# Attention with sinks and a gated network on one core: the sinks' product in 64 weight columns, late value products reordered, a new step order

## The chip, the cores and the metric

One core of one Trainium2 chip runs the whole program. The metric is the device time of one execution in microseconds (us). The kernel before took 727.1 us, the median of 3 runs (726.25 to 728.53).

## The reference

```python
scores = scale * np.matmul(q, k.transpose(0, 1, 3, 2))      # 4 batches, 8 heads, 768 x 64
keep = is_sink | in_window                                  # first 4 keys, or the last 128
a = np.exp(np.where(keep, scores, -1e9) - max); a = a / (sum + 1e-9)
attn_out = np.matmul(a, v)
x = attn_out.transpose(0, 2, 1, 3).reshape(3072, 512)
h = x @ w_in                                                # 512 x 2048
out = (h * np.cos(h)) @ w_out                               # 2048 x 512
```

All of it is fp32; the weights arrive as 64-bit floats.

## The kernel before, in words

Every fp32 product that needs accuracy is made of three fast products: an operand is split into a rounded high part and a rest (fp32r), and high x high, high x low and low x high are summed in PSUM.

The 768 query rows of a batch are worked in chunks of 256 rows (`CB` = 2 blocks of 128). `chunks` lists first the four chunks at row 0 (the early heads, 32 of them: chunk and head), then the other two chunks of each batch (the late heads, 64 of them, 16 for each batch). Two chunks make a pair, and each of the 6 pairs then goes through the dense network in 16 slots (`dense_pair`): 12 matmuls of 512 columns into `h` (L476), sine and gate on ACT and DVE, 12 matmuls into `acc` (L521).

A late head takes scores against its window blocks and 8 sink keys (L1024), a mask with the row minimum (L1046), an exponential (L1055), a normalisation (L1075), a transpose of the probabilities (L1136), a split into high and low (L1162, L1167) with two triangular selections on POOL (L1174), and the value product `values` (L1215). That one is 7 matmuls into one PSUM tile `av` of 128 x 256. The stationary operand (the weights, loaded by LDWEIGHTS, on rows PEld) is the value block: 128 columns (`v` high and `v` low side by side) against the high probabilities, or its 64 high columns against the low ones. The moving operand has 256 columns for the key block that both query blocks see (wide) and 128 for the two others (narrow). In the order of before: wide high, the sinks, narrow high, narrow low, wide low, narrow high, narrow low.

The sinks' matmul serves 4 heads from one moving tile `gt`: `sink_cols` (L1105, L1107) gathers the sinks' probabilities of 4 heads into 16 rows each, high and low; `sink_turn` transposes (L1120) and `sink_out` copies to `gt`. Its weights `sink_values()` lie in the tile `x1r`. Each batch makes them once: `load_batch_v` (L852 to L861) issues 8 DMAs from SP into `xb`, and `vs_part` (L1091, four times) splits them with two DVE (or POOL) instructions each. `xb` is one buffer: the low half of each late head's value product also goes through it (`x_low` L1222, `x_sum` L1234), so a batch's load starts after the `x_sum` of the head before, and the first head's `x_low` comes after the four `vs_part`.

The order is not written by hand. Each step is added with engines and guessed durations, dependencies, buffers and a priority worked out from constants in `C`; `Plan.order` plays a list schedule and emits the instructions in its order of starts. Each engine then runs its own list in order. A load of 4 planner units (`dma(4)`) counts 1.8 us of SP there, and a `vs_part` 0.55 us of DVE. In gaps of the plan PE gets filler matmuls (`fill`, L1532, up to 60).

Of the kernel before, what the change touches and what calls it, by code (L numbers as in the profile page):

```python
# [9 lines left out]
F32 = mybir.dt.float32  # L10
# [8 lines left out]
SW = P + NSINK  # L19
GR = 96 + 2 * NSINK  # L20
BW = 2 * P + NSINK
# [5 lines left out]
C = {  # L27
# [4 lines left out]
    "POOLF": 0.999, "POOLPEN": 2.492, "R": 2, "RAW": 2, "SAME": 0.056, "SEM": 0.352, "SPE": -0.019, "STEP": 7.601,  # L32
# [3 lines left out]
}  # L36
# [136 lines left out]
def attn_moe_kernel(ctx, tc, q, k, v, n_sink, window, w_in, w_out, out):  # L173
# [50 lines left out]
    neg3 = cp.tile([P, 4], F32, name="neg")  # L224
    neg, quarter = neg3[:, 0:2], neg3[:, 2:3]
    lims = cp.tile([1, 2, 2, 2], F32, name="lims")
# [6 lines left out]
    def setup():  # L233
# [8 lines left out]
        nc.gpsimd.iota(rc_i[:, 0], pattern=[[-1, P]], base=0, channel_multiplier=1)  # L242
        nc.gpsimd.iota(rc_i[:, 1], pattern=[[1, P]], base=0, channel_multiplier=0)
        nc.vector.memset(ones, 1.0)
        nc.vector.memset(quarter, HALF_PI_DOWN)
# [9 lines left out]
        nc.vector.tensor_single_scalar(out=minus, in_=ident, scalar=-1.0, op=ALU.mult)  # L255
        nc.vector.tensor_copy(out=rc, in_=rc_i)
        nc.vector.tensor_single_scalar(out=env.below, in_=rel, scalar=0.0, op=ALU.is_lt)

# [537 lines left out]
    def banded_path(ctx2):  # L796
# [33 lines left out]
        def x1r():  # L830

            if env.x1r is None:
                env.x1r = ap.tile([P, NP * NT], F32R, name="x1r", tag="x1")
                env.vs = env.x1r.rearrange("p (a b c d) -> p a b c d", a=NP, b=2, c=2)
            return env.x1r
# [16 lines left out]
        def load_batch_v(o):  # L852
            def fn(e):
                o.vs32 = xb[:, : 2 * D].rearrange("p (n d) -> p n d", d=D)
                for h in range(4):
                    for dup in range(2):
                        r0 = h * 32 + dup * 8
                        nc.sync.dma_start(
                            out=o.vs32[r0 : r0 + 8], in_=v[o.b, h::4, 0:NSINK, :].rearrange("p s d -> s p d")
                        )  # L860
            return fn  # L861
# [229 lines left out]
        def vs_part(o, h):  # L1091
            def fn(e):
                w = sink_values().rearrange("p (g a) b c d -> p g (a b) c d", g=2)
                r = slice(h * 32, h * 32 + 2 * NSINK)
                e.tensor_copy(out=w[r, :, h, 0, :], in_=o.vs32[r])
                e.tensor_tensor(
                    out=w[r, :, h, 1, :], in0=o.vs32[r], in1=f32(w)[r, :, h, 0, :], op=ALU.subtract
                )
            return fn

        def sink_cols(o, four):
            def fn(e):
                j0 = o.sj[0]
                for h, oo in enumerate(four):
                    nc.vector.tensor_copy(out=gc.bitcast(F32R)[:, j0:, h * 32 : h * 32 + NSINK], in_=oo.p[:, j0:, P:SW])  # L1105
                for h, oo in enumerate(four):
                    nc.vector.tensor_tensor(  # L1107
                        out=gc[:, j0:, h * 32 + NSINK : h * 32 + 2 * NSINK], in0=oo.p[:, j0:, P:SW],
                        in1=gc[:, j0:, h * 32 : h * 32 + NSINK], op=ALU.subtract,
                    )  # L1110
            return fn
# [4 lines left out]
        def sink_turn(o):  # L1116
            def fn(e):
                o.gp = late_bank(o, 2)[:GR]
                for n, j in enumerate(o.sj):
                    nc.tensor.transpose(  # L1120
                        out=o.gp[:, n * P : (n + 1) * P], in_=gc[:, j], identity=ident,
                    )
            return fn

        def sink_out(o):
            def fn(e):
                w = len(o.sj) * P
                copy(e, gt[:GR, :w], o.gp[:, :w])
            return fn
# [66 lines left out]
        def values(o):  # L1196


            def fn(e):
                o.av = late_bank(o, 1)  # L1200
                mms = {}
                for t, w in ((o.phi, 2 * D), (o.plo, D)):
                    for n, (kb, qs) in enumerate(o.cols):
                        dst = o.av[:w, (qs[0] - o.i0) * P : (qs[-1] + 1 - o.i0) * P]
                        lhs = o.vr[:, kb - o.kb0].rearrange("p a d -> p (a d)")[:, :w]
                        mms.setdefault((w, len(qs)), []).append((dst, lhs, t[:, o.offs[n] * P : o.offs[n + 1] * P]))
                (wide_hi,), (wide_lo,) = mms[2 * D, CB], mms[D, CB]
                narrow = [m for pair in zip(mms[2 * D, 1], mms[D, 1]) for m in pair]
                seq = [wide_hi]
                if o.sj:  # L1210
                    lhs = sink_values()[:, o.pair, o.odd].rearrange("p a d -> p (a d)")
                    seq.append((o.av[:, o.sj[0] * P :], lhs, gt[:, : len(o.sj) * P]))
                seq += [*narrow[:2], wide_lo, *narrow[2:]]
                for n, (dst, lhs, rhs) in enumerate(seq):
                    nc.tensor.matmul(  # L1215
                        out=dst, lhsT=lhs, rhs=rhs, start=(n == 0), stop=(n == len(seq) - 1), skip_group_check=True
                    )
# [64 lines left out]
        def before_softmax(g, o):  # L1282
# [35 lines left out]
            if o.early:  # L1318
                if o.odd == 0:
# [3 lines left out]
                    i = add(dma(2), load_natural(xq_t, src, CB), [bx], pq, lat=2.3 if g else 1.9)  # L1323
                    i = qt = add([("PE", 0.23)], pe_turn(o, 0, xq_t, CB), [i, bb], t - 6 * T + C["DQ"] + 0.3)
                    bx.users.append(i)
# [105 lines left out]
        def after_softmax(g, o):  # L1431
            x, t = xs[o.a], head_time(g)
            if o.first is o:
                o.bv, o.bvs = buf("xb", 1), buf("vs", 1)
                i = add(dma(4), load_batch_v(o), [o.bv], t - 3 * T, lat=2.3)
                d = [i, o.bvs]
# [256 lines left out]
        ps = env.ps = ctx2.enter_context(tc.tile_pool(name="ps", bufs=1, space=PSUM))  # L1693
        gc = ap.tile([P, CB, GR], F32, name="gc")
        env.x1f = ap.tile([P, NP, PT], F32, name="x1f", tag="x1")
# [157 lines left out]
```

## Time and profile before

| what | before |
|---|---|
| median of 3 runs | 727.1 us |
| span of the profiled execution, first to last instruction | 725.6 us |
| PE (matmul) busy | 708.8 us, 98% |
| DVE, ACT, POOL busy | 599.3, 527.7, 127.5 us |
| granted clock of PE | 0.999 |

The trace counts from the first instruction. The profiled execution's own time is not given apart from its span; the span is 1.5 us below the median of the runs. A matmul's end in the trace is modelled, and matmuls overlap, so a matmul's cost is read from the distance between its start and the next one's start.

### The profile page before, as it was taken

The page shows a single profiled execution, that of the slowest core. Times are in us where ns is not written, and L with a number is a line of the kernel's source. Part 1 is how long each engine was busy: PE and PEld are TensorE (multiplying, and loading weights), DVE is VectorE, ACT ScalarE, POOL GpSimd, SP SyncE. Part 2 cuts the span into 40 slices and gives each one's busy share as a digit, 9 for nine tenths or more (in the row PEclk, how much of TensorE's full clock was granted, in tenths as well). Part 3 has the DMA queues.
Part 4 walks back from the last instruction along what each step waited for, and adds up shares of the span by engine and source line. Part 5 has one row for each costly group of instructions (what it writes and reads, how often), then busy time and mean ns, then how long its engine had stood idle before and what let it go on. Part 6 is the DMA issues. An engine that isn't in the chain of part 4 may idle for free.

```text
span 725.6 us, 12986 instructions
## 1 busy us (share of the span) xinstructions
PE 708.8 (98%) x3674; PEld 584.1 (81%) x3674; DVE 599.3 (83%) x1849; ACT 527.7 (73%) x1344; POOL 127.5 (18%) x213
## 2 busy tenths in 40 slices
PE   7998999999999999999999999999999999999996
PEld 7766787888888888888888888888888888888884
DVE  6889998988988978988978988878989865667762
ACT  3896976788697697796686886776887766566642
POOL 1010000001223222232231222232123222100000
PEclk9999999999999999999999999999999999999999
DMA  5665555533256333355433254433254500375551
GB/s 144 182 186 153 158 162 162 141 65 68 68 118 146 73 62 57 72 119 124 93 60 59 56 131 103 118 61 64 43 139 99 119 18 12 97 210 148 164 137 64
DMA packets 236501, 77.13 MB, mean 106 GB/s; under 512 B 221060, under 2 KB 221060, under 8 KB 236420
## 3 DMA queue, kind: packets, MB, share of 16 engines
q1 hardware_dynamic: 236128, 75.15, 43.4%
q10 hardware_dynamic: 292, 1.05, 0.5%
q8 instruction: 32, 0.52, 0.3%
q14 instruction: 49, 0.40, 0.2%
HBM read 69.86 MB, written 6.29 MB: 105 GB/s over the span
## 4 chain that ended last, share of the span: by engine, by line
PE 81%; ACT 11%; DVE 4%; issue 2%; DMA 1%; SPq 0%; ACTq 0%; DVEq 0%
PE acc L521 32%; PE h L476 32%; PE av L1215 5%; PE s L1024 4%; ACT p L1055 3%; PE s L968 2%; PE av L1191 2%; PE tp L1136 2%; ACT p L1073 1%; PE tp L1146 1%; PE qk L931 1%; ACT L485 1%; PE idle L1532 1%; ACT L1055 1%; ACT early L390 1%
## 5 line engine op out<-in xcount | busy, mean ns | idle before, releaser
L521 PE MATMUL acc<-whi_out,ghi 128*128 128x512 f32 x384 | 161.8, 421 | 0.0
L476 PE MATMUL h<-xhi,whi_in 128*128 128x512 f32 x384 | 155.2, 404 | 0.0
L476 PE MATMUL h<-xlo,whi_in 128*128 128x512 f32 x384 | 150.9, 393 | 0.0
L521 PE MATMUL acc<-whi_out,glo 128*128 128x512 f32 x384 | 150.8, 393 | 0.0
L521 PE MATMUL acc<-wlo_out,ghi 128*128 128x512 f32 x384 | 150.1, 391 | 0.0
L476 PE MATMUL h<-xhi,wlo_in 128*128 128x512 f32 x384 | 150.0, 391 | 0.0
L1174 POOL TENSOR_SCALAR_AFFINE_SELECT ph<-ph 128x512 fp32r<-128x512 f32 x128 | 87.4, 683 | 230.3 <-DVE ph L1167 226.4
L485 ACT ACTIVATE r<-h 128x512 f32<-128x512 f32 x96 | 57.1, 598 | 48.6 <-PE h L476 46.0
L476 PEld LDWEIGHTS h<-xlo,whi_in 128*128 128x128 f32 x384 | 72.1, 188 | 16.3
L521 PEld LDWEIGHTS acc<-whi_out,glo 128*128 128x128 f32 x384 | 72.1, 188 | 16.2
L476 PEld LDWEIGHTS h<-xhi,whi_in 128*128 128x128 f32 x384 | 72.2, 188 | 12.0 <-DVE r L498 0.3
L476 PEld LDWEIGHTS h<-xhi,wlo_in 128*128 128x128 f32 x384 | 72.4, 189 | 11.2
L521 PEld LDWEIGHTS acc<-whi_out,ghi 128*128 128x128 f32 x384 | 72.8, 190 | 10.7
L521 PEld LDWEIGHTS acc<-wlo_out,ghi 128*128 128x128 f32 x384 | 72.7, 189 | 9.4
L1055 ACT ACTIVATE p<-p,st 128x136 f32<-128x136 f32 (+1 forms) x192 | 79.2, 416 | 0.3
L498 DVE SCALAR_TENSOR_TENSOR r<-r,h 128x512 f32<-128x512 f32 x96 | 64.6, 674 | 16.9 <-ACT r L491 16.1
L506 ACT CAST ghi<-r 128x512 fp32r<-128x512 f32 x96 | 59.5, 619 | 22.8 <-PE acc L521 15.7
L512 DVE TENSOR_TENSOR glo<-r,ghi 128x512 fp32r<-128x512 f32 x96 | 66.3, 691 | 7.1 <-ACT ghi L506 6.3
L1046 DVE CUSTOM_DVE_ANT_0 p<-s,mk 128x136 f32<-128x136 f32 (+1 forms) x192 | 59.8, 313 | 6.5 <-PE s L968 3.1
L984 ACT CAST l<-tq 64x256 fp32r<-64x256 f32 x64 | 25.8, 403 | 46.7 <-PE s L1024 46.4
L1032 DVE COPY_PREDICATED s<-mk,s 128x128 f32<-128x128 int32 x128 | 37.3, 291 | 24.6 <-PE s L1024 22.5
L1024 PEld LDWEIGHTS s<-r,l 128*128 128x128 f32 x256 | 46.5, 188 | 12.3 <-DVE ph L1167 1.5
(153 smaller groups left out, 1302.3 us busy)
## 6 DMA issues: line engine op xcount, KB each, us to landing
xk<-in_k_dram SPq DMA_DIRECT2D x256, 48.0 KB
raw<-in_moe_w_out_dram SPq DMA_DIRECT2D x16, 512.0 KB
wt<-in_moe_w_in_dram SPq DMA_DIRECT2D x32, 256.0 KB
raw<-in_moe_w_in_dram SPq DMA_DIRECT2D x14, 512.0 KB
v<-in_v_dram SPq DMA_DIRECT2D x64, 96.0 KB
raw<-in_v_dram SPq DMA_DIRECT2D x32, 192.0 KB
out_dram<-wt SPq DMA_DIRECT2D x22, 256.0 KB
wt<-in_moe_w_out_dram SPq DMA_DIRECT2D x20, 256.0 KB
```

The costliest lines, as they stand in the source:

```text
L476: nc.tensor.matmul(out=o.h, lhsT=w[:, c, fs], rhs=xx[:, c, :], start=(c == 0 and n == 0), stop=(c == NC - 1 and n == 2),)
L485: nc.scalar.activation(out=o.r, in_=o.h, func=AF.Sin, scale=0.5)
L498: nc.vector.scalar_tensor_tensor(out=o.r, in0=o.r, scalar=0.5, in1=o.h, op0=ALU.subtract, op1=ALU.mult)
L506: nc.scalar.copy(out=o.ghi, in_=o.r)
L512: e.tensor_tensor(out=o.glo, in0=o.r, in1=f32(o.ghi), op=ALU.subtract)
L521: nc.tensor.matmul(out=y.acc[j], lhsT=gg[:, j * P : (j + 1) * P], rhs=w[:, f, :], start=(f == 0 and n == 0), stop=(f == NFT - 1 and n == 2),)
L1024: nc.tensor.matmul(out=o.s_ps[j][:, :w], lhsT=o.l[:, j * P : (j + 1) * P], rhs=r.rearrange("p n s -> p (n s)")[:, c0 : c0 + w], start=(n = ...
L1032: nc.vector.copy_predicated(out=o.s_ps[j][:, :P], mask=below.bitcast(I32), data=o.s_ps[j][:, SW : SW + P])
L1046: nc.vector.tensor_tensor_reduce(out=o.pj[j][:, :w], in0=o.s_ps[j][:, :w], in1=masks[min(o.i0 + j, 2)][:, :w], op0=ALU.add, op1=ALU.min, s ...
L1055: nc.scalar.activation(out=o.pj[j][:, :w], in_=o.pj[j][:, :w], func=AF.Exp, bias=o.lead.st[:, 0, o.nth, j : j + 1], scale=-1.0, accum_out= ...
L1174: nc.gpsimd.affine_select(out=ph[:, :, b, :], in_=f32(ph)[:, :, 1, :], pattern=[[0, 2 * CB], [(-1, 1)[b], P]], compare_op=(ALU.is_gt, ALU. ...
L1215: nc.tensor.matmul(out=dst, lhsT=lhs, rhs=rhs, start=(n == 0), stop=(n == len(seq) - 1), skip_group_check=True)
```

## The change

1. `vs_part` and `load_batch_v`: the values of the sinks stand in 4 copies instead of 2 (16 DMAs of 8 rows for a batch, before 8). Of each head's 32 rows, 16 hold the high part and 16 the rest; both lie in the same 64 columns. `vs_part` takes 3 instructions on 32 rows instead of 2 on 16. Setup makes the sign that it needs (`odd16`).
2. `sink_cols` writes each probability part twice (32 rows for each head); `gc` has 128 columns instead of 112, and the transposes and copies cover 128 rows.
3. `values`: the sinks' weights have 64 columns instead of 128, and the order is narrow high, narrow low, sinks, narrow high, narrow low, wide low, wide high.
4. The load of the first batch's sink values depends on the last early pair's q transposes on PE.
5. Most of the planner's constants in `C` have new values.

```diff
             def fn(e):
                 o.vs32 = xb[:, : 2 * D].rearrange("p (n d) -> p n d", d=D)
                 for h in range(4):
-                    for dup in range(2):
+                    for dup in range(4):
...
         def vs_part(o, h):
             def fn(e):
-                w = sink_values().rearrange("p (g a) b c d -> p g (a b) c d", g=2)
-                r = slice(h * 32, h * 32 + 2 * NSINK)
-                e.tensor_copy(out=w[r, :, h, 0, :], in_=o.vs32[r])
-                e.tensor_tensor(
-                    out=w[r, :, h, 1, :], in0=o.vs32[r], in1=f32(w)[r, :, h, 0, :], op=ALU.subtract
-                )
+                r = slice(h * 32, h * 32 + 32)
+                w = sink_values()[r, :, h // 2, h % 2, :]
+                e.tensor_copy(out=w, in_=o.vs32[r])
+                e.tensor_scalar(out=w, in0=f32(w), scalar1=odd16[r], scalar2=1.0, op0=ALU.mult, op1=ALU.mult)
+                e.tensor_tensor(out=w, in0=f32(w), in1=o.vs32[r], op=ALU.add)
...
-                (wide_hi,), (wide_lo,) = mms[2 * D, CB], mms[D, CB]
-                narrow = [m for pair in zip(mms[2 * D, 1], mms[D, 1]) for m in pair]
-                seq = [wide_hi]
-                if o.sj:
-                    lhs = sink_values()[:, o.pair, o.odd].rearrange("p a d -> p (a d)")
-                    seq.append((o.av[:, o.sj[0] * P :], lhs, gt[:, : len(o.sj) * P]))
-                seq += [*narrow[:2], wide_lo, *narrow[2:]]
+                sinks = o.av[:D], sink_values()[:, o.h // 4, o.pair % 2, o.odd], gt
+                seq = [
+                    block(0, o.phi, 2 * D), block(0, o.plo, D), sinks, block(2, o.phi, 2 * D),
+                    block(2, o.plo, D), block(1, o.plo, D), block(1, o.phi, 2 * D),
+                ]
...
-                    i = qt = add([("PE", 0.23)], pe_turn(o, 0, xq_t, CB), [i, bb], t - 6 * T + C["DQ"] + 0.3)
+                    i = qt = env.turned = add([("PE", 0.23)], pe_turn(o, 0, xq_t, CB), [i, bb], t - 6 * T + C["DQ"] + 0.3)
...
-                i = add(dma(4), load_batch_v(o), [o.bv], t - 3 * T, lat=2.3)
+                i = add(dma(4), load_batch_v(o), [o.bv] + ([env.turned] if o.b == 0 else []), t - 3 * T, lat=2.3)
...
-    "DV": 0.57, "DX": 4.638, "FILL": 60, "CV": 1.947, "CL": 15.777, "HO": -18.522, "SX": -5.15, "CR": 9.813,
+    "DV": 0.435, "DX": 5.298, "FILL": 60, "CV": 9.941, "CL": 26.879, "HO": -25.153, "SX": -5.111, "CR": 8.062,
...
-    "T": 6.724, "TH": 7.177, "WARM": 5, "WARM2": 0, "P0": 12.442, "A0": -3.102, "D0": 9.766, "G0": 3.059,
+    "T": 6.674, "TH": 7.389, "WARM": 5, "WARM2": 0, "P0": 13.606, "A0": -4.046, "D0": 12.406, "G0": -0.285,
...
-    "WO": 8.749, "WS": 1.523, "WS2": 1.141, "WT": 2, "XV": 2, "VP": 3.149,
+    "WO": 9.561, "WS": 0.201, "WS2": 1.447, "WT": 2, "XV": 2, "VP": -8.681,
```

`VP` shifts the priority of `vs_part`, `HO` that of all late heads; no guessed duration of a changed step has a new value.

## Rows read from the trace of the kernel before

**Rows 1.** The page: busy us, share of the span and instructions of each engine.
```profile
PE 708.8 (98%) x3674; PEld 584.1 (81%) x3674; DVE 599.3 (83%) x1849; ACT 527.7 (73%) x1344; POOL 127.5 (18%) x213
```
**Rows 2.** Stages: length, busy us of PE, PEld, DVE, ACT, POOL; clock, DMA, GB/s.
```profile
0.00:20.00 20.00, 16.15 (x87) 14.98 (x88) 14.15 (x54) 5.86 (x16) 2.51 (x13) 1.00 0.57 152
20.00:40.00 20.00, 18.56 (x117) 15.29 (x116) 17.83 (x62) 18.53 (x64) 1.21 (x2) 1.00 0.68 179
40.00:60.00 20.00, 18.32 (x96) 13.54 (x95) 17.86 (x59) 17.82 (x58) 1.89 (x2) 1.00 0.65 174
60.00:80.00 20.00, 18.59 (x89) 14.06 (x88) 18.69 (x47) 14.25 (x34) 0.31 (x1) 1.00 0.55 155
...
200.00:300.00 100.00, 99.68 (x532) 82.77 (x531) 86.47 (x290) 78.77 (x210) 26.53 (x42) 1.00 0.41 86
...
600.00:700.00 100.00, 100.00 (x467) 82.21 (x467) 67.25 (x159) 60.96 (x119) 6.92 (x9) 1.00 0.50 135
700.00:726.00 26.00, 19.11 (x85) 15.09 (x83) 8.64 (x25) 8.45 (x14) 0.00 (x0) 0.95 0.20 61
```
**Rows 3.** The page: shares of the span in the chain that ended last, by engine.
```profile
PE 81%; ACT 11%; DVE 4%; issue 2%; DMA 1%; SPq 0%; ACTq 0%; DVEq 0%
```
**Rows 4.** Fillers: ns min/median/max, first and last start; then busy us.
```profile
L1532 PE MATMUL idle<-gt x60: 278/362/775, 5.0 to 31.1; 128*128 128x256 f32 x60
...
L1532 PE MATMUL idle<-gt 128*128 128x256 f32 x60 | 13.8, 360 | 0.0
```
**Rows 5.** The sinks' matmul of all late heads: ns min/median/max, first and last start.
```profile
L1215 PE MATMUL av<-gt,x1r x64: 278/279/285, 188.7 to 619.7; 128*128 128x256 f32 x64
```
**Rows 6.** PE by time, first late head's value product: start us, us, what.
```profile
188.87 0.52 PE L1215 MATMUL av<-ph,vr 128*128 128x128 f32 x5
189.23 0.44 PE L521 MATMUL acc<-whi_out,ghi 128*128 128x512 f32 x1
189.51 0.40 PE L521 MATMUL acc<-wlo_out,ghi 128*128 128x512 f32 x1
189.74 0.40 PE L521 MATMUL acc<-whi_out,glo 128*128 128x512 f32 x1
```
**Rows 7.** PE in order of time, behind the last late head's value product.
```profile
620.14 0.44 PE L521 MATMUL acc<-whi_out,ghi 128*128 128x512 f32 x1
620.42 0.40 PE L521 MATMUL acc<-wlo_out,ghi 128*128 128x512 f32 x1
```
**Rows 8.** PE by time, dense matmuls behind a scores pair (264 columns).
```profile
304.27 0.40 PE L1024 MATMUL s<-r,l 128*128 128x264 f32 x2
304.50 0.40 PE L476 MATMUL h<-xhi,whi_in 128*128 128x512 f32 x1
304.74 0.40 PE L476 MATMUL h<-xhi,wlo_in 128*128 128x512 f32 x1
```
**Rows 9.** Weight loads of value products by shape: busy us, mean ns.
```profile
L1215 PEld LDWEIGHTS av<-ph,vr 128*128 128x128 f32 x192 | 36.2, 189 | 0.6
L1215 PEld LDWEIGHTS av<-ph,vr 128*64 128x64 f32 x192 | 21.1, 136 | 0.0
```
**Rows 10.** SP's issues by time, at the start and at the second batch.
```profile
10.27 3.74 SPq L858 DMA_DIRECT2D yt<-in_v_dram  x8
14.53 0.91 SPq L923 DMA_DIRECT2D xq<-in_q_dram  x2
...
291.86 3.16 SPq L858 DMA_DIRECT2D yt<-in_v_dram  x8
```
**Rows 11.** DVE by time: the second batch's sink values, first and last.
```profile
296.59 0.66 DVE L1095 CAST x1r<-yt 16x128 fp32r<-16x128 f32 x1
...
299.92 0.23 DVE L1095 CAST x1r<-yt 16x128 fp32r<-16x128 f32 x1
300.18 0.29 DVE L1096 TENSOR_TENSOR x1r<-yt,x1r 16x128 fp32r<-16x128 f32 x1
```
**Rows 12.** PE in order of time, the value product that needs those sink values.
```profile
300.39 0.40 PE L521 MATMUL acc<-whi_out,glo 128*128 128x512 f32 x1
300.62 0.28 PE L1215 MATMUL av<-ph,vr 128*128 128x256 f32 x1
```

More of the change, by code (lines that the diff above doesn't have):

```diff
@@ L19 @@
 SW = P + NSINK
-GR = 96 + 2 * NSINK
 BW = 2 * P + NSINK
@@ L27 @@
 C = {
[4 rows of a table removed]
-    "POOLF": 0.999, "POOLPEN": 2.492, "R": 2, "RAW": 2, "SAME": 0.056, "SEM": 0.352, "SPE": -0.019, "STEP": 7.601,
[3 rows of a table removed]
[3 rows of a table added]
+    "GLO": 2, "L": 1, "LAG": 3.448, "LEAD": 35.415, "NM": 5.093, "NW": 3.472, "NWF": 0.49, "PB": 5, "PEN": 19.889,
+    "POOLF": 1.105, "POOLPEN": 0.934, "R": 2, "RAW": 2, "SAME": 0.055, "SEM": 0.352, "SPE": -0.028, "STEP": 7.679,
[3 rows of a table added]
 }
@@ L224, in attn_moe_kernel @@
     neg3 = cp.tile([P, 4], F32, name="neg")
-    neg, quarter = neg3[:, 0:2], neg3[:, 2:3]
+    neg, quarter, odd16 = neg3[:, 0:2], neg3[:, 2:3], neg3[:, 3:4]
     lims = cp.tile([1, 2, 2, 2], F32, name="lims")
@@ L243, in setup @@
         nc.gpsimd.iota(rc_i[:, 1], pattern=[[1, P]], base=0, channel_multiplier=0)
+        nc.gpsimd.iota(odd16.bitcast(I32), pattern=[[0, 1]], base=0, channel_multiplier=1)
         nc.vector.memset(ones, 1.0)
@@ L256, in setup @@
         nc.vector.tensor_copy(out=rc, in_=rc_i)
+        nc.vector.tensor_scalar(
+            out=odd16.bitcast(I32), in0=odd16.bitcast(I32), scalar1=4, scalar2=1,
+            op0=ALU.logical_shift_right, op1=ALU.bitwise_and,
+        )
+        nc.vector.tensor_single_scalar(out=odd16, in_=odd16.bitcast(I32), scalar=-1.0, op=ALU.mult)
         nc.vector.tensor_single_scalar(out=env.below, in_=rel, scalar=0.0, op=ALU.is_lt)
@@ L833, in x1r @@
                 env.x1r = ap.tile([P, NP * NT], F32R, name="x1r", tag="x1")
-                env.vs = env.x1r.rearrange("p (a b c d) -> p a b c d", a=NP, b=2, c=2)
+                env.vs = env.x1r[:, : NP * 2 * D].rearrange("p (g a o d) -> p g a o d", g=2, o=2, d=D)
             return env.x1r
@@ L1102, in fn @@
             def fn(e):
-                j0 = o.sj[0]
+                g5 = gc.rearrange("p j (h r c s) -> p j h r c s", r=2, c=2, s=NSINK)
                 for h, oo in enumerate(four):
-                    nc.vector.tensor_copy(out=gc.bitcast(F32R)[:, j0:, h * 32 : h * 32 + NSINK], in_=oo.p[:, j0:, P:SW])
+                    nc.vector.tensor_copy(
+                        out=g5.bitcast(F32R)[:, :, h, :, 0],
+                        in_=oo.p[:, :, P:SW].unsqueeze(2).broadcast_to([P, CB, 2, NSINK]),
+                    )
                 for h, oo in enumerate(four):
                     nc.vector.tensor_tensor(
-                        out=gc[:, j0:, h * 32 + NSINK : h * 32 + 2 * NSINK], in0=oo.p[:, j0:, P:SW],
-                        in1=gc[:, j0:, h * 32 : h * 32 + NSINK], op=ALU.subtract,
+                        out=g5[:, :, h, :, 1], in0=oo.p[:, :, P:SW].unsqueeze(2).broadcast_to([P, CB, 2, NSINK]),
+                        in1=g5[:, :, h, :, 0], op=ALU.subtract,
                     )
@@ L1117, in fn @@
             def fn(e):
[L1118 to L1122, printed above, removed]
+                o.gp = late_bank(o, 2)
+                for j in range(CB):
+                    nc.tensor.transpose(out=o.gp[:, j * P : (j + 1) * P], in_=gc[:, j], identity=ident)
             return fn
@@ L1126, in fn @@
             def fn(e):
-                w = len(o.sj) * P
-                copy(e, gt[:GR, :w], o.gp[:, :w])
+                copy(e, gt, o.gp)
             return fn
@@ L1200, in fn, with block @@
                 o.av = late_bank(o, 1)
[L1201 to L1206, printed above, removed]
-                (wide_hi,), (wide_lo,) = mms[2 * D, CB], mms[D, CB]
-                narrow = [m for pair in zip(mms[2 * D, 1], mms[D, 1]) for m in pair]
-                seq = [wide_hi]
-                if o.sj:
-                    lhs = sink_values()[:, o.pair, o.odd].rearrange("p a d -> p (a d)")
-                    seq.append((o.av[:, o.sj[0] * P :], lhs, gt[:, : len(o.sj) * P]))
-                seq += [*narrow[:2], wide_lo, *narrow[2:]]
+                def block(n, t, w):
+                    kb, qs = o.cols[n]
+                    return (
+                        o.av[:w, (qs[0] - o.i0) * P : (qs[-1] + 1 - o.i0) * P],
+                        o.vr[:, n].rearrange("p a d -> p (a d)")[:, :w], t[:, o.offs[n] * P : o.offs[n + 1] * P],
+                    )
+                sinks = o.av[:D], sink_values()[:, o.h // 4, o.pair % 2, o.odd], gt
[3 more added lines that the diff above has]
+                ]
                 for n, (dst, lhs, rhs) in enumerate(seq):
@@ L1693, in banded_path @@
         ps = env.ps = ctx2.enter_context(tc.tile_pool(name="ps", bufs=1, space=PSUM))
-        gc = ap.tile([P, CB, GR], F32, name="gc")
+        gc = ap.tile([P, CB, P], F32, name="gc")
         env.x1f = ap.tile([P, NP, PT], F32, name="x1f", tag="x1")
```

8 rows, old and new, of the table C are left out of this document.

## The prediction

> **What bounds the kernel now.** I read the page's busy times first: PE is busy for 708.8 of 725.6 us, and nothing else is near it [rows 1]. A share of the whole span hides stages, so I cut the span into stages next [rows 2]. From 200 to 300 us PE is busy for 99.68 of 100 us and DVE for 86.47; from 600 to 700 PE has no gap at all. The only stages in which PE has room are the first 80 us (16.15, 18.56, 18.32 and 18.59 of 20 us, so 8.4 us idle together) and the end (19.11 of 26, the last stores). To the 8.4 us belong the 60 filler matmuls, 13.8 us busy, all between 5.0 and 31.1 us [rows 4]: they are work for nobody. The chain that ended last agrees: 81% of it is PE, 11% ACT, 4% DVE [rows 3].
>
> So there are two ways to a shorter time. Between about 190 and 620 us, where the late heads lie among dense slots, a nanosecond that PE saves is a nanosecond of the end, as long as DVE (86%) keeps up. In the first 80 us only a better order helps. A busy PE can still be slow, so the third view is the distance from one matmul's start to the next one's.
>
> **The change part by part.**
>
> *The order of the value product.* In the first late head the five last matmuls (narrow high, narrow low, wide low, narrow high, narrow low) start at 188.87, and the next dense one at 189.23: 0.36 us for 768 moving columns, so about 0.06 us for a narrow matmul of 128 and 0.12 for a wide one of 256 (4 x 0.06 + 0.12 = 0.36). Nothing is lost there. But the dense matmul that follows at 189.23 has its successor only at 189.51, 0.28 us later, while the next step is 0.23 [rows 6]. The last late head shows the same 0.28 (620.14 to 620.42) [rows 7]. Behind the scores pair, whose last matmul has 264 columns, the dense matmul at 304.50 takes its usual 0.24 [rows 8]. So it isn't the change from attention to dense that costs, but what stands just before: a narrow matmul of 0.06 us is too short a cover for the dense matmul's weights of 128 columns. A load of 128 columns lasts 189 ns in the trace and one of 64 columns 136 [rows 9]; both contain a fixed part, and the 53 ns between them are the price of 64 columns, so 128 columns need about 106 ns, of which 0.06 us is covered and some 0.05 is not. That is the excess (0.28 - 0.23 = 0.05).
>
> After the change the last matmul is wide (0.12 us), and behind it the dense weights are covered as behind the scores. I go through the new order for a new hole of the same kind: narrow high's 128 columns stand behind whatever preceded the head (at least 0.12 us in rows 6 and 8); narrow low's 64 columns (53 ns) behind a narrow one (0.06); the sinks' 64 columns behind narrow low (0.06), which 128 columns would not have fitted; narrow high's 128 behind the sinks (0.12); narrow low and wide low have 64 each, behind narrow ones; wide high's 128 behind wide low. No hole is left. The matmuls themselves stay: 4 x 0.06 + 3 x 0.12 before and after, since a step follows the moving columns. There are 64 late heads, from 188.7 to 619.7 us [rows 5], all in stages in which PE is full: 64 x 0.052 = **-3.3 us**. (0.052 lies between 0.04 and 0.06, the roundings of these rows: -2.6 to -3.8.) The sinks' product in 64 columns saves nothing by itself; it lets this order close.
>
> The Trainium skill, page "TensorE: Matmul & The Clock Gate", section "LDWEIGHTS (loading the stationary operand)", says that a load takes its number of columns divided by 1.2 in ns: 107 and 53 ns here. The trace's difference of 53 ns agrees, and by that rule the sum would be 64 x (107 - 60) = 3.0 us. Another section of that page, "Step-by-step: what each phase is for", speaks against the change: PE pulls loads ahead of matmuls in flight when they go to the background weight buffer. By it the narrow tail would hide the dense load too, and the sum would be 0.
>
> *More work for sinks.* The transposes of the gathered sinks go from 112 to 128 columns, 2 for each group of 4 heads, 32 in all; 16 columns at 53/64 ns are 13 ns, so at most 0.4 us, hidden under a dense matmul: 0. `sink_cols` doubles 16 elements to 32 in 128 instructions and `vs_part` gets a third instruction, 16 x about 0.28 = 4.5 us (the last of these rows) [rows 11], so some 6 us on DVE in 430 us in which it has 13.5% idle [rows 2]: 0 on the path by itself, up to 6 us if DVE became the bound. I take 0.
>
> *The load of the sinks' values.* For the first batch 8 DMAs hold SP from 10.27 to 14.01 us [rows 10]; 16 would have held it to 17.8, over the q load at 14.53. The change puts them behind the early heads' transposes, more than 100 us later, with the use only near 185 us. The q load at 14.53 comes 0.5 us after SP was free, so SP was not what held it: the edit by itself gives 0, at most the 3.7 us. The other three batches are in the crowded part: 8 DMAs take 3.16 us of SP, so 0.395 each; 16 take 6.3, that is 3.2 us more, and 3 x 8 of them are new. This lies in a chain with no slack, as the third rival tells; in the forecast the new order hides it.
>
> *Setup.* One iota on POOL and two tiny DVE instructions beside waits of setup for DMA and PE: 0, at most 0.5 us.
>
> *The new order.* What it does can't be read from constants. It could take at most the 8.4 us of idle and 13.8 us of fillers in the first 80 us, 22 us, of which most is the length of the first heads' chain and stays. It can lose as easily: DVE is at 18.69 of 20 us from 60 to 80 us, and what is put ahead of an early head's mask there delays PE directly. Where PE is full it can only lose. I take 0, and +-3 us (a third of the idle of the first 80 us) for the range.
>
> Sum on the profiled execution: 725.6 - 3.3 = 722.3 us of span. The median of the runs lies 1.5 us over the span, so **723.8 us**, 0.46% faster than 727.1.
>
> **The rivals.**
>
> *A: the order also closes part of the start.* PE idles 8.4 us and fills 13.8 us there; if a fifth of the 22 us goes too, 4.4 us, the time is 719.4. For: DVE and ACT, not PE, pace that part (17.83 and 18.53 of 20 from 20 to 40 us), and SP loses 3.74 us of issues from its middle. Against: nothing shows a single large wait that a reorder would remove.
>
> *B: the 0.05 us stays.* If weights are loaded well before the matmul ahead of them starts, the narrow tail isn't what costs 0.05 us, and the excess has another origin that the order inside the product doesn't touch. (The Trainium skill's rule on loads pulled ahead, above, says so.) Then PE's work is what it was, and the time is 727.1, within 1.5. For it speaks only that the trace shows no stall marked on those matmuls; against it the comparison of rows 6 and 8.
>
> *C, slower: the sink values come too late in three batches.* The batch's load can't start before the head before has freed `xb`; at the second batch it is issued at 291.86, is used from 296.59 on, the last part ends at 300.47, and the value product that needs it starts at 300.62, directly behind a dense matmul at 300.39 [rows 10 to 12]. So there is 0.15 us between the last instruction and its reader, about what a handover takes, and no slack. Now 8 more DMAs (3.2 us) and four more instructions of about 0.28 us (1.1 us) stand in this chain, 4.3 us, and the planner still counts 1.8 us for the load and 0.55 for a part. The value product is in PE's list at a fixed place, with all dense work behind it waiting. If the new order puts no more than before between load and product, PE stands for 4.3 us in each of three batches: 723.8 + 12.9 = 736.7. It decides from the point where the other work that the order puts ahead of that product is less than these 4.3 us; half covered gives 730.2. For: rows 10 to 12, and unchanged guesses. Against: dense work is at hand at any time there, and only its place in the list must change.
>
> **How the numbers follow.** The forecast has 0.47, A 0.17, B 0.16 and C 0.20. A run of this kernel can tell about 0.3% (2.2 us) from no change: below 724.9 is faster, above 729.3 slower. The forecast's own range, with +-3 us for the order, is 721 to 727, three quarters of it faster; A is faster; B is the same; C is slower in nine parts of ten. Faster 0.47 x 0.8 + 0.17 + 0.03 = 0.58; same 0.47 x 0.2 + 0.13 + 0.02 = 0.24; slower 0.18. The range reaches into A to 717.5 and into C to its half-covered time and a little more, 731.5.
>
> **What would show it.** Right: the value products' wide high matmul stands last and the dense matmul behind it has a step of 0.23 us; the span from the first to the last late head is about 3 us shorter; weight loads of 64 columns number 256 there. Wrong: steps of 0.28 behind value products (B); a gap on PE ahead of the first value product of a batch, released by the sink values or their DMA (C); PE's idle and fillers of the first 80 us changed by more than 3 us either way (A, or its opposite).

## The result, and the profile after

The changed kernel takes 736.9 us (median of 4 runs, 736.49 to 738.17), the kernel before beside it 727.3: a ratio of 1.0134, 95% interval 1.0122 to 1.0146. It is 9.6 us slower, where 3.3 us less were forecast, and outside the stated range of 717.5 to 731.5. The profiled execution took 738.17 us with a span of 736.4.

The page after: span and busy times of the engines.
```profile
span 736.4 us, 13073 instructions
...
PE 709.1 (96%) x3674; PEld 580.8 (79%) x3674; DVE 598.3 (81%) x1886; ACT 533.7 (72%) x1333; POOL 134.5 (18%) x206
```
PE is busy for as long as before (709.1 against 708.8 [rows 1]) in a span 10.8 us longer. So PE did not get more work, it stands idle longer. The stages say where (length; busy us of PE, PEld, DVE, ACT, POOL; clock; DMA share; GB/s).
```profile
60.00:80.00 20.00, 16.35 (x68) 12.38 (x69) 16.32 (x42) 14.29 (x36) 1.77 (x2) 0.91 0.54 158
...
0.00:80.00 80.00, 68.62 (x371) 56.60 (x372) 64.40 (x217) 58.18 (x177) 5.86 (x18) 0.98 0.60 165
80.00:190.00 110.00, 107.22 (x531) 85.26 (x530) 99.56 (x270) 82.10 (x206) 7.98 (x12) 1.00 0.46 116
190.00:610.00 420.00, 414.96 (x2229) 342.13 (x2228) 355.95 (x1206) 323.86 (x818) 113.04 (x165) 1.00 0.39 84
```
The same three stretches of the kernel before:
```profile
0.00:80.00 80.00, 71.61 (x383) 57.86 (x384) 68.53 (x221) 56.45 (x170) 5.92 (x18) 1.00 0.61 165
80.00:190.00 110.00, 109.25 (x552) 88.73 (x551) 101.14 (x284) 84.52 (x211) 5.29 (x10) 1.00 0.47 116
190.00:610.00 420.00, 418.82 (x2247) 348.48 (x2246) 360.26 (x1185) 324.18 (x848) 112.85 (x181) 1.00 0.40 86
```
PE lost 3.0, 2.0 and 3.9 us of busy time there, and from 60 to 80 us its granted clock averages 0.91 where it was 1.00 [rows 2].

**The hole is gone, as foretold.** PE in order of time, the last late head's value product and what follows it:
```profile
628.29 0.52 PE L1219 MATMUL av<-ph,vr 128*128 128x128 f32 x4
628.65 0.39 PE L526 MATMUL acc<-whi_out,ghi 128*128 128x512 f32 x1
628.88 0.40 PE L526 MATMUL acc<-wlo_out,ghi 128*128 128x512 f32 x1
```
The dense matmul behind the product has a step of 0.23 us, where [rows 7] had 0.28. But the second sign of being right failed: from the first to the last late head (start of the sinks' matmul) it is 438.0 us where it was 430.9 [rows 5], 7.1 longer instead of 3 shorter.

**Early, PE waits for score masks, and then runs at the lower clock.** PE by time from 67 to 75 us; in brackets the idle time before an instruction and what ended it.
```profile
67.79 0.49 PE L973 MATMUL s<-tk,early 128*128 128x128 f32 x2
68.78 0.70 PE L973 MATMUL s<-tk,early 128*128 128x256 f32 x2 [0.50 <-DVE st L1051]
71.13 0.44 PE L936 MATMUL qk<-ident,xq 128*128 128x128 f32 x2 [1.65 <-DVE st L1051]
...
72.32 0.63 PE L481 MATMUL h<-xhi,wlo_in 128*128 128x512 f32 x1
72.74 0.63 PE L481 MATMUL h<-xlo,whi_in 128*128 128x512 f32 x1
...
75.16 0.39 PE L481 MATMUL h<-xlo,whi_in 128*128 128x512 f32 x1
```
The next scores, and the transposes of q behind them, stand until DVE's mask (L1051) has read the scores before them, 0.50 and 1.65 us. Behind that the dense steps are 0.43 us instead of 0.23: the lower of the two clock levels, 1.2 GHz, for 3.4 us, which cost some 1.5 us.

**At each later batch PE waits 1.3 to 1.5 us for a mask that stands behind the sink values.** DVE by time at the second batch (L1100 to L1102 are the three instructions of one part of the sink values):
```profile
305.86 0.48 DVE L1100 CAST x1r<-yt 32x128 fp32r<-32x128 f32 x1
306.38 0.27 DVE L1101 TENSOR_SCALAR x1r<-x1r,neg 32x128 fp32r<-32x128 f32 x1
306.68 0.28 DVE L1102 TENSOR_TENSOR x1r<-x1r,yt 32x128 fp32r<-32x128 f32 x1
...
309.33 0.29 DVE L1102 TENSOR_TENSOR x1r<-x1r,yt 32x128 fp32r<-32x128 f32 x1
309.64 0.30 DVE L1037 COPY_PREDICATED s<-mk,s 128x128 f32<-128x128 int32 x1
309.97 0.42 DVE L996 TENSOR_TENSOR l<-tq,l 64x256 fp32r<-64x256 f32 x1
310.42 0.30 DVE L1051 CUSTOM_DVE_ANT_0 p<-s,mk 128x136 f32<-128x136 f32 x1
```
PE beside it: the sinks' matmul that uses these sink values, and what follows:
```profile
308.92 0.28 PE L1219 MATMUL av<-gt,x1r 128*64 128x256 f32 x1
309.04 0.52 PE L1219 MATMUL av<-ph,vr 128*128 128x128 f32 x4
310.88 0.41 PE L1140 MATMUL tp<-ident,p 128*128 128x128 f32 x2 [1.32 <-DVE st L1051]
```
Four parts of three instructions are one block of 3.8 us, without a gap, so DVE did not wait for the 16 DMAs. The value product itself is in time: its sinks' matmul starts at 308.92, even before the block's last instruction (309.33), since the weights of one head come from one of the four parts. What comes late is the mask behind the block. In the kernel before, the parts had two instructions and the masks stood between them:
```profile
297.28 0.73 DVE L1096 TENSOR_TENSOR x1r<-yt,x1r 16x128 fp32r<-16x128 f32 x1
297.94 0.28 DVE L1032 COPY_PREDICATED s<-mk,s 128x128 f32<-128x128 int32 x1
...
298.47 0.28 DVE L1046 CUSTOM_DVE_ANT_0 p<-s,mk 128x136 f32<-128x136 f32 x1
...
298.79 0.22 DVE L1095 CAST x1r<-yt 16x128 fp32r<-16x128 f32 x1
```

**At the end a chain has moved behind the dense work.** `most_t` (a transpose on PE) begins a chain of small steps on PE and DVE that ends in `redo`, the flag on which all engines branch at the end. PE before (the last line is the last dense matmul), then PE and DVE's last instruction after:
```profile
708.92 0.27 PE L1651 MATMUL most_t<-ident,most 128*33 128x128 f32 x1
...
718.72 0.39 PE L521 MATMUL acc<-whi_out,glo 128*128 128x512 f32 x1
```
```profile
727.59 0.39 PE L526 MATMUL acc<-whi_out,glo 128*128 128x512 f32 x1
727.82 0.27 PE L1655 MATMUL most_t<-ident,most 128*33 128x128 f32 x1
```
```profile
729.71 0.15 DVE L1677 SCALAR_TENSOR_TENSOR redo<-row_t,sm 1x1 int32<-1x1 f32 x1
```
The chain ran beside dense work and now runs behind it. From the last dense matmul's start to the end of the span it is 8.85 us instead of 6.85. This comes with the new order: the eight profiled kernels of this document that have the new constants take 8.8 to 9.2 us there, the nine that have the old ones 6.6 to 7.0.

### The profile page after: what moved, and what is told of

Read it like the earlier page. It is cut to its first block, busy times and chain, and to the rows that moved or that the text cites. A ratio compares the mean times of both kernels' runs of the same rounds, so it can differ in the third digit from the quotient of the medians.

```text
span 736.4 us, 13073 instructions
## 1 busy us (share of the span) xinstructions
PE 709.1 (96%) x3674; PEld 580.8 (79%) x3674; DVE 598.3 (81%) x1886; ACT 533.7 (72%) x1333; POOL 134.5 (18%) x206
## 4 chain that ended last, share of the span: by engine, by line
PE 74%; DVE 10%; ACT 9%; DMA 3%; issue 2%; SPq 0%; DVEq 0%; ACTq 0%
PE h L481 29%; PE acc L526 27%; PE av L1219 5%; PE s L1029 4%; PE s L973 2%; ACT p L1060 2%; PE av L1195 2%; PE tp L1140 2%; ACT p L1078 1%; ACT early L395 1%; DMA xq<-in_q_dram 1%; DVE wt L594 1%; DVE glo L517 1%; DVE p L1051 1%; DMA xk<-in_k_dram 1%
## 5 line engine op out<-in xcount | busy, mean ns | idle before, releaser
L526 PE MATMUL acc<-whi_out,ghi 128*128 128x512 f32 x384 | 158.9, 414 | 0.0
L1051 DVE CUSTOM_DVE_ANT_0 p<-s,mk 128x136 f32<-128x136 f32 (+1 forms) x192 | 59.9, 313 | 9.9 <-PE s L973 5.4
L517 DVE TENSOR_TENSOR glo<-r,ghi 128x512 fp32r<-128x512 f32 x89 | 62.1, 701 | 3.5 <-ACT ghi L511 3.0
L1029 PEld LDWEIGHTS s<-r,l 128*128 128x128 f32 x256 | 43.8, 188 | 20.4 <-DVE ph L1171 5.7
L1029 PE MATMUL s<-r,l 128*128 128x264 f32 x256 | 55.1, 296 | 2.2 <-DVE l L996 1.3
```

What stands on the lines that cost most here:

```text
L517: e.tensor_tensor(out=o.glo, in0=o.r, in1=f32(o.ghi), op=ALU.subtract)
L526: nc.tensor.matmul(out=y.acc[j], lhsT=gg[:, j * P : (j + 1) * P], rhs=w[:, f, :], start=(f == 0 and n == 0), stop=(f == NFT - 1 and n == 2),)
L1029: nc.tensor.matmul(out=o.s_ps[j][:, :w], lhsT=o.l[:, j * P : (j + 1) * P], rhs=r.rearrange("p n s -> p (n s)")[:, c0 : c0 + w], start=(n = ...
L1051: nc.vector.tensor_tensor_reduce(out=o.pj[j][:, :w], in0=o.s_ps[j][:, :w], in1=masks[min(o.i0 + j, 2)][:, :w], op0=ALU.add, op1=ALU.min, s ...
```

## The experiments

Times are medians; behind them stands the ratio to the kernel before on the same chip with its 95% interval. "The distance of two batches" is the time from the 17th sinks' matmul to the 49th, 32 late heads: before 300.74 to 525.12, 224.4 us; after 308.92 to 535.40, 226.5 us.

**Code and order apart.** The changed code with the constants of before:
```diff
-    "ALT": 1.239, "BLF": 0.824, "CK": 41.153, ...   (all of C)
+    "ALT": 1.986, "BLF": 0.62, "CK": 43.221, ...
```


> The changed code with the constants of before, so with the old step order (the first batch's load still waits for the early heads). Theory: the slowdown of 9.6 us is the new order's (about 6 us before 190 us, 1 us at the end) and a longer block of sink-value instructions on DVE in three batches (1.5 us each); the new value product itself gives -3.3 us. With the old order the early loss is gone, and only the four extra DVE instructions of a batch (1.1 us) can come late: 727.3 - 3.3 + 0 to 3.4, so 724 to 727.5, middle 726. Rival C of the prediction (load and instructions together stand in the chain, 4.3 us a batch, in any order): 736.7. Rival B (the reordered product gives nothing): 727 to 731.

761.6, 1.0463 (1.0444 to 1.0482), outside all three forecasts. This separates nothing: the new dependency of the first load moves the whole list schedule, and PE waits 5.8, 3.1 and 2.8 us in single places of the late heads. Without that dependency the order is that of before:
```diff
-                i = add(dma(4), load_batch_v(o), [o.bv] + ([env.turned] if o.b == 0 else []), t - 3 * T, lat=2.3)
+                i = add(dma(4), load_batch_v(o), [o.bv], t - 3 * T, lat=2.3)
```


> As the changed code with the constants of before, but without the dependency of the first batch's load on the early heads: 16 DMAs on SP within the first 20 us. Theory: SP is held from about 10.3 to 17.5 us, the q and k loads of the third early pair start some 3 us late and PE has no other work there: 1 to 3.3 us more than with the dependency. Rival: the loads of that stage are hidden anyway: the same time as with the dependency.

733.1, 1.0077 (1.0063 to 1.0091): 28 us less than with the dependency, where neither forecast had less. PE's matmuls stand in the very order of before, and the new code alone costs 5.9 us, though its holes are gone (dense step behind a value product 0.23 us). In the trace the dense work is 2.3 us late from its first matmul on, and each of the four batches adds about 1 us. And the code of before under the new constants and dependency:

> The code of before with the constants of after, and with the first batch's load behind the early heads as in after, so the new step order alone. Theory: the early loss (6 us) and that of the end (1 us) are all here; the batches' stalls of 1.5 us go, since a sink-value part has two instructions; the hole behind the narrow tail costs its 3.3 us again: 736.9 - 4.6 + 3.3, so about 735.5, range 733 to 737.5. Rival C (the loss is the added sinks' work): 727 to 730.

733.1, 1.0078 (1.0064 to 1.0091): the new order alone costs 5.8 us. Its stages show PE's busy time short by 3.7 and 1.3 us ahead of 190 us; in the late heads PE is as full as before. The rest is at the end, behind the last dense matmul's start: 9.1 us instead of 6.9.
```profile
0.00:80.00 80.00, 67.95 (x374) 55.73 (x375) 65.13 (x216) 58.93 (x177) 5.76 (x17) 0.98 0.61 165
80.00:190.00 110.00, 107.92 (x535) 86.04 (x534) 100.45 (x270) 82.35 (x207) 8.96 (x13) 1.00 0.47 117
190.00:610.00 420.00, 419.29 (x2245) 348.37 (x2244) 353.48 (x1210) 327.54 (x827) 112.44 (x164) 1.00 0.39 83
```

**The changed kernel with one part taken back.** The old sequence of the seven value matmuls:
```diff
-                    block(0, o.phi, 2 * D), block(0, o.plo, D), sinks, block(2, o.phi, 2 * D),
-                    block(2, o.plo, D), block(1, o.plo, D), block(1, o.phi, 2 * D),
+                    block(1, o.phi, 2 * D), sinks, block(0, o.phi, 2 * D), block(0, o.plo, D),
+                    block(1, o.plo, D), block(2, o.phi, 2 * D), block(2, o.plo, D),
```


> The kernel after with the seven matmuls of a late head's value product in the sequence of before (wide high, sinks, narrow high, narrow low, wide low, narrow high, narrow low), the sinks still with 64 weight columns. Theory: the 0.05 us behind each narrow tail comes back, 47 of the 64 products have a dense matmul behind them at once: 2.4 to 3.3 us more, 739.3 to 740.2. Rival B (the order of the product doesn't matter): 736.9.

739.6, 1.0161 (1.0142 to 1.018): the new sequence is worth some 2.8 us there; from the first to the last late head the traces have 440.7 us here and 438.0 in the changed kernel. The sink values in two instructions instead of three, with the same result:
```diff
-                e.tensor_copy(out=w, in_=o.vs32[r])
-                e.tensor_scalar(out=w, in0=f32(w), scalar1=odd16[r], scalar2=1.0, op0=ALU.mult, op1=ALU.mult)
+                e.tensor_scalar(out=w, in0=o.vs32[r], scalar1=odd16[r], scalar2=1.0, op0=ALU.mult, op1=ALU.mult)
```


> The kernel after with two instructions instead of three in a sink-value part: the first copy is dropped, since the product with minus one or zero rounds to the same value. Theory: in the late heads' part PE waits because DVE's list is longer by the sinks' work (per batch 4 instructions of about 0.28 us in the parts, 0.35 us in the gathers), and a DVE us costs almost a PE us there: 4 x 0.25 to 0.3 us less for each of 3 to 4 batches, -3 to -4.5 us: 732.5 to 734, and the distance between the same instruction of two batches falls from 113.2 to about 112.2 us. Rival (the 16 DMAs on SP make the values late): 736.9, within 0.5.

734.4, 1.011 (1.0094 to 1.0125), and the distance falls to 224.4 us. PE's waits from 190 to 610 us (line, awaited tile and line: us in total, times, longest), first of the changed kernel, then of this one:
```profile
PE tp L1140 <- DVE st L1051: 4.2, 3, 1.5
PE s L1029 <- DVE ph L1171: 0.8, 3, 0.3
```
```profile
PE s L1029 <- DVE ph L1170: 0.8, 3, 0.3
PE tp L1139 <- DVE st L1051: 0.8, 3, 0.3
```
One small instruction less in each part: DVE's busy time falls from 598.3 to 593.8 us, the block of a batch from 3.8 to 2.7 us, and 3.4 us of PE's waits go. Then 8 DMAs of 32 rows instead of 16 of 8:
```diff
-                    for dup in range(4):
-                        r0 = h * 32 + dup * 8
+                    for n in range(2):
                         nc.sync.dma_start(
-                            out=o.vs32[r0 : r0 + 8], in_=v[o.b, h::4, 0:NSINK, :].rearrange("p s d -> s p d")
+                            out=o.vs32[h * 32 : h * 32 + 32, n],
+                            in_=v[o.b, h + 4 * n, 0:NSINK, :].unsqueeze(0).broadcast_to([4, NSINK, D]),
```


> The kernel after with 8 DMAs instead of 16 for a batch's sink values (each fills 32 rows by reading the same 8 rows four times); everything else as after. Theory: the values are not what DVE waits for, its parts start without a gap before them: 736.4 to 736.9. Rival (SP's 2.7 us more for each batch are the price): 3 x 1.5 us or more less, 732.5 or below.

735.5, 1.0122 (1.0106 to 1.0137), the distance 226.6 us as in the changed kernel: the DMAs of the later batches are hidden. The 1.4 us that the time is lower lie within the two intervals. And the first batch's load without its dependency:

> The kernel after without the dependency of the first batch's load on the early heads. Theory: a list schedule isn't stable; one dependency changes the place of many steps (with the old constants it made 28 us between two kernels of the same code), so the constants of after fit only the plan with it, and without it the time is several us longer, 740 to 765. Rival: the dependency only moves that load, so only the first 20 us change: 736.9 with a change within 3 us.

735.3, 1.0114 (1.0098 to 1.0129): the theory missed, the rival held. The dependency that moved 28 us under the old constants moves under 2 here.

**The code with these mends in the old order.** Two instructions, 8 DMAs, constants of before:

> The changed code with the old order, the first batch's load at the start (733.1 us as it stands), and both mends: two instructions in a part, 8 DMAs for a batch. Theory: the start gets back 2.35 us (PE waited for the q load of the third pair that SP issued late), each of 3 to 4 batches 1.0 to 1.2 us, so 726 to 727.5; against before, the reordered product gives -2.7 to -3.3 and the wider gathers take 1.4, so it should be 0 to 1.5 us faster than before. Rival (the stalls of the batches have another cause than instructions and DMAs of the sinks): 730.8.

729.2, 1.003 (1.0019 to 1.004), slower than the theory's 726 to 727.5: the 8 wider DMAs still hold SP from 10.13 to 15.67 us, and the dense work starts 1.2 us late. Then the same with the first batch's load moved behind the key load of the first late head:
```diff
         def load_k(o): ...
+                if o.first is o and o.b == 0:
+                    load_batch_v(o, True)(e)
```


> The changed code in the order of before with the sink values written by two instructions and loaded by 8 DMAs (729.2 when the first batch's load stood in the kernel's first 20 us), and now the first batch's load is issued behind the key load of the first late head. Theory P: TensorE's late start of that kernel (1.2 to 1.4 us late at 24 us) goes with the load: 727.5 to 728. Theory D says the same of the start; the late heads stay where they were. If the start was not the load's doing: 729.2 again.

734.5, 1.0097 (1.0081 to 1.0113): a miss for both theories. The start did recover, but the 8 DMAs now stand ahead of a weight load on SP, DVE stands for the weights with the masks behind them, and PE for DVE; behind the wait PE's granted clock is 0.57 from 151 to 155 us. SP, DVE and PE by time:
```profile
138.02 5.92 SPq L864 DMA_DIRECT2D yt<-in_v_dram  x8
144.06 0.38 SPq L573 DMA_DIRECT2D raw<-in_moe_w_out_dram  x1
```
```profile
147.81 0.43 DVE L588 TENSOR_SCALAR wt<-raw 128x512 int32<-128x512 int32 x1 [5.83 <-DMA raw<-in_moe_w_out_dram]
```
```profile
151.42 0.48 PE L1153 MATMUL tp<-ident,p 128*128 128x128 f32 x1 [5.04 <-DVE early L397]
```
So I issued them one at a time, one behind each early head's value load:
```diff
         def load_v(o): ...
+                if o.early and env.parts:
+                    env.parts.pop()()
```


> The changed code in the old order with two instructions and 8 DMAs (729.2), the first batch's 8 DMAs now issued one at a time, one behind the value load of each early head, so that nowhere more than one of them stands ahead of other loads on SP. If the start's 1.2 us and the 5.2 us wait of the moved load (734.5) are both a matter of how many DMAs stand in one place of SP's queue: 728.0, and no wait of TensorE over 1.5 us between 8 and 160 us. If not: 729.2 or more.

727.9, 1.001 (1.0 to 1.002): as expected, and no wait of PE over 1.2 us between 8 and 190 us is left.

**The value sequence by itself, in the kernel before.**
```diff
-                seq = [wide_hi]
+                seq = [hi0, lo0]
                 if o.sj:
-                    lhs = sink_values()[:, o.pair, o.odd].rearrange("p a d -> p (a d)")
-                    seq.append((o.av[:, o.sj[0] * P :], lhs, gt[:, : len(o.sj) * P]))
-                seq += [*narrow[:2], wide_lo, *narrow[2:]]
+                    lhs = sink_values()[:, o.pair, o.odd, 0]
+                    seq.append((o.av[:D, o.sj[0] * P :], lhs, gt[:, : len(o.sj) * P]))
+                seq += [hi1, lo1, wide_lo, wide_hi]
```


> The kernel before, its own step order and its own loads, gathers and 112-column transposes; only the seven value matmuls stand in the new sequence, and the sinks' matmul uses the 64 columns of the high halves (the low halves of the sink values are left out, so it adds nothing on DVE). Theory P (TensorE alone sets the late heads' pace, as the prediction had it): all 64 holes of 0.05 us go and so does their time, 3.3 us: 724.0, and the distance of two batches falls from 224.4 us to 222.7. Theory D (DVE's list runs as close as TensorE, so what TensorE saves comes back as waits for probabilities, score copies or masks): the steps behind the value products fall to 0.23 us, but the distance stays at 223.8 to 224.4 us and the time at 726 to 727.3.

725.2, 0.9972 (0.9957 to 0.9987): faster than both kernels, by 2.1 us against before, but without the low halves of the sink values. It lies between the theories. The distance is 223.9 us, so of the 1.6 us that 32 holes hold, 0.5 arrived in this stretch. PE's waits from 190 to 610 us, before and here:
```profile
PE tp L1136 <- DVE st L1046: 0.8, 4, 0.2
```
```profile
PE tp L1136 <- DVE st L1046: 1.1, 4, 0.3
PE tp L1136 <- ACT p L1073: 0.7, 3, 0.2
```
The holes closed in full: PE's instructions stand in the same order, and the 64 dense steps behind value products fall from 0.282 to 0.234 us on average, 3.1 us together. But from the first to the last late head only 1.1 us is left of it (429.9 against 430.9). About 1.0 us has turned into the waits listed, most of them for ACT's probabilities, not for DVE, and about as much into longer steps around transposes and scores. Another 0.7 us of this trace's lead stands ahead of the first late head (188.0 against 188.7 us), where the edit changes nothing, so that is chance; the interval of the runs, 0.9 to 3.1 us, is the safer figure. With DVE's work cut instead, and with both edits (the gathers' low halves left out):
```diff
         def sink_cols(o, four): ...
-                for h, oo in enumerate(four):
-                    nc.vector.tensor_tensor(out=gc[:, j0:, h * 32 + NSINK : h * 32 + 2 * NSINK], ..., op=ALU.subtract)
```


> The kernel before with one thing less on DVE: the gathers' low halves (four subtractions per four heads, about 0.7 us of DVE each time, 11 us in all) are left out, and those columns stay zero. Value products as before. Theory P: DVE is no bound, 727.3 as before, within 0.7. Theory D: TensorE's small waits on DVE in each batch (some 0.3 to 0.5 us a batch) go: 725 to 726.5, and the distance of two batches falls by up to 1 us.

> Both edits in the kernel before: value matmuls in the new sequence with the high halves of the sinks alone, and the gathers' low halves left out. Theory P: as the value sequence alone, 724.0. Theory D: only now does the sequence's 3.3 us show, 722 to 724, clearly under the value sequence alone (726 to 727.3).

727.5, 0.9998 (0.9987 to 1.001), and 725.3, 0.9963 (0.995 to 0.9977). The edit took 4.3 us off DVE (599.3 to 595.0; the 11 us of the expectation were too many), about what the third instruction had put on it, and the times show no gain from it; both theories for the second run (724.0, or 722 to 724) missed. So the 3.3 us aren't held back by DVE's sum of work, and theory D falls in that form. A smaller part isn't excluded: from the first to the last late head the traces have 430.4 us with the gathers cut and 428.8 with both edits, 0.5 and 1.0 less than without the cut, while three runs with one and the same code in the late heads (729.2, 734.5 and 727.9) differ there by 0.8.

**Do the sums add?** The sequence alone (same edit) with the old code under the new order, and the changed kernel with all three mends:

> The old code under the new order (733.1) with the value matmuls alone in the new sequence and the sinks' matmul on the high halves only (the low halves of the sink values are left out), so without a single added DVE instruction. Theory S (the order's cost and the sequence's gain are separate sums): 5.8 us above before less the 2.1 us that the sequence gave in the old order: 731.0, between 730.3 and 731.7. Theory I (the new order has its own bound, so the sequence gives nothing there): 733 again. The waits for score masks near 68 us stand as in the changed kernel under both.

731.5, 1.0066 (1.0048 to 1.0084): the order's cost and the sequence's gain add, within the interval. From the first to the last late head the two traces have 434.9 and 432.9 us.

> The changed kernel with the sink values written by two instructions, loaded by 8 DMAs of 32 rows, and the first batch's load free of its wait. Each of these alone gave 2.5, 1.4 and 1.6 us. Theory S (they add): 736.9 less 5.5 = 731.4. Theory O (what the two smaller ones gave was the same thing twice, the early stretch at the low clock or its waits, and only the third instruction is a cost of the late heads): 733 to 734.4.

734.2, 1.0103 (1.0088 to 1.0117): no better than two instructions alone (734.4), so the smaller two mends are not further sums.

## Why the prediction was wrong

The way from 727.3 to 736.9 in four steps, each the difference of two runs' distances from before, and by their intervals uncertain by some 1.5 us: the new order +5.8 (old code, new order); the value sequence -1.3 in that order (5.8 to 4.5); the sinks' wider code in its cheapest form, without the dependency, +2.6 (4.5 to 7.1); its third instruction, 16 DMAs and dependence +2.5 (7.1 to 9.6).

- *The new order: "I take 0, and +-3 us".* This is the largest miss: the order alone costs 5.8 us, and rival A falls with it. What I wrote beside it, that a mask put back in DVE's list from 60 to 80 us delays PE directly, is what happened: 2.2 us of waits near 69 us, and behind them the lower clock (some 1.5 us). The third piece stands where I didn't look: I gave the new order only the first 80 us to work in and read the end as "the last stores", but the chain that ends in `redo` moved behind the last dense matmul, 2.2 us in that run. Other early waits changed too (for `xhi` of ACT from 0.4 to 2.2 us), so how the 5.8 us add up isn't shown in full. A schedule that I couldn't read deserved a range of the order of the 8.4 us of idle, to both sides, and I gave it a third.
- *More work for sinks: "0 on the path by itself, up to 6 us if DVE became the bound".* It failed, and the reason that I gave for 0 failed with it. The amount was right: the new order alone has 593.0 us of DVE, the changed kernel 598.3, so 5.3 us for the "some 6". But DVE is no busier than before (599.3 us), and 4.3 us less of the gathers gained under 1 us, while 4.5 us less of the sink values gave 2.5 us of time. What counts is whether an instruction stands ahead of a mask that PE is about to need. The parts that I put at 0 cost 2.6 + 2.5 us. The instructions themselves are as small as estimated (busy us, mean ns):
```profile
L1102 DVE TENSOR_TENSOR x1r<-x1r,yt 32x128 fp32r<-32x128 f32 x16 | 4.5, 282 | 0.6
L1101 DVE TENSOR_SCALAR x1r<-x1r,neg 32x128 fp32r<-32x128 f32 x16 | 4.5, 279 | 0.6
```
- *The value product, -3.3.* The mechanism was right, a 0.05 us hole behind a narrow tail that a wide tail closes; rival B falls (3.1 us of steps closed, and putting back the old sequence alone cost some 2.8 us). The size in time was not: 2.1 us alone, 1.3 to 2.8 in the other surroundings. "A nanosecond that PE saves is a nanosecond of the end, as long as DVE (86%) keeps up" was the wrong step: PE at 99.7% still has ACT and DVE a few tenths of a us behind it, and once it is faster it meets them. In the late heads of that trace 2.0 of the 3.1 us came back, about half of it as listed waits.
- *The load of the sink values.* For the later batches the cost is 0, as forecast. For the first the working held too. "SP was not what held it" is borne out for the 8 DMAs: with none of them in a block there (727.9) the q load goes out at 13.84 us instead of 14.53, and the dense work starts no earlier. And 16 at the start, forecast to hold SP to 17.8 us over the q load, hold it to 17.25 instead of 14.01 [rows 10] in the old order: the q load comes 2.8 us later, and PE starts at 44.47 us the matmul (`av` from `xhi`) that it started at 42.12. SP's issues of the kernel with the changed code in the old order:
```profile
10.06 7.19 SPq L863 DMA_DIRECT2D yt<-in_v_dram  x16
17.36 0.91 SPq L928 DMA_DIRECT2D xq<-in_q_dram  x2
```
- *Rival C* gave 736.7 and the time is 736.9, but by another way, so the agreement is luck. Its place was right (DVE's extra instructions at three batches), its victim was not: the sink values came in time and a mask behind them did not, for 1.3 to 1.5 us a batch instead of 4.3. The "no slack" of [rows 10 to 12] was a misreading: the sinks' matmul needs one part, not the last of four (after the change it starts before the last one has ended), and that it stood 0.15 us behind the last one was chance.

What stays open: which of the constants puts the early scores so that PE waits near 69 us, whether `CE`, which shifts the last chain's place and goes from -3.976 to -1.476, alone puts it behind the dense work (no run changed them one by one), and which piece of the wider sinks' code (gathers of 32 columns, transposes of 128, parts of 32 rows) makes up the 2.6 us that its cheapest form costs in the new order and the 2.7 us in the old one (727.9 against 725.2).

## What to carry to other kernels

Price an added instruction by what stands behind it in its engine's list at that moment, not by the engine's idle share: 4.5 us of DVE work in blocks ahead of a mask cost 2.5 us of time, and 4.3 us of it elsewhere under 1 us. A DMA issue is an instruction of its queue too; the same eight cost 1.3 us more at the start (729.2) and 6.7 us more ahead of a weight load (734.5) than one by one (727.9). And when an edit comes together with a new schedule, take the edit alone into the old one first: here the sequence by itself was worth 2.1 us, the same sequence with the sinks' wider code nothing (727.9 at best), and the schedule that came with it cost 5.8. Look at the end of such a schedule as well as at its middle: a chain of 2 us that nothing covers any more costs 2 us.

## What the runs showed that was not expected

The lower clock comes after almost the same waits in one profiled execution and not in another. In the changed kernel with two instructions the waits near 69 us are the same 0.50 and 1.65 us, yet the dense steps behind them stay at 0.23 us:
```profile
68.10 0.70 PE L973 MATMUL s<-tk,early 128*128 128x256 f32 x2 [0.50 <-DVE st L1051]
70.45 0.44 PE L936 MATMUL qk<-ident,xq 128*128 128x128 f32 x2 [1.65 <-DVE st L1051]
...
71.39 0.40 PE L481 MATMUL h<-xhi,wlo_in 128*128 128x512 f32 x1
71.62 0.39 PE L481 MATMUL h<-xlo,whi_in 128*128 128x512 f32 x1
```
That profiled execution (731.9 us, granted clock 0.996 over the span) was the fastest of its runs; the other three took 734.1 to 736.0 at 0.994 and 0.995. What decides it wasn't tried; for a sum it means that a wait of 2 us can cost 1.5 us more than itself.
